# Leftover keys in four row groups, second weights' sums from their pieces, and a new order of the work

## The chip, the cores and the metric

The kernel runs on one core of a Trainium2 chip. The metric is the device time of one execution in microseconds. A core has TensorE (PE, with its weight loads shown apart as PEld), VectorE (DVE), ScalarE (ACT), GpSimd (POOL) and SyncE (SP), which here issues nearly all DMAs. Of TensorE's two clock levels, 1.2 and 2.4 GHz, this profile shows the upper one, a granted clock of 1.0, in every stretch.

## The reference

Attention over pooled keys and values, then a two-layer feed-forward with an own activation:

```python
# q, k, v: (8, 8, 576, 64) float32
k_p = k.reshape(B, H, 72, 8, D).mean(axis=3)          # 576 keys pooled by 8 to 72
v_p = v.reshape(B, H, 72, 8, D).mean(axis=3)
scores = q @ k_p.transpose(0, 1, 3, 2) / 8
attn = exp(scores - max); attn = attn / (attn.sum(-1) + 1e-9)
x = (attn @ v_p).transpose(0, 2, 1, 3).reshape(4608, 512)
h = x @ w_in                                           # (4608, 2048)
sp = maximum(h, 0) + log1p(exp(-abs(h)))
out = (h * erf(sp)) @ w_out                            # (4608, 512)
```

## The kernel before, in words

**Chunks and units.** The 4608 tokens are nine chunks of 512. A chunk's attention is made in two units of 256 tokens, 18 units in all; a unit is two tiles of 128 tokens. 576 tokens of a batch are no multiple of 256, so a unit may hold tokens of two batches (`parts`); those units read two sets of values.

**Precision.** Feed-forward operands are split into a high and a low part (`halves`, L460 and L472: `hi` is rounded, `lo` is the rest), and a product is three matmuls (`three`, L834: hi·hi, hi·lo, lo·hi). `pairs` issues them with 512 moving columns.

**A unit of attention.** `softmax_tile` makes the scores (L663), the softmax, and transposes the probabilities (L708). The 72 keys of a head are 64 plus 8 left over. The 64 of every head go through `pa` into `et`; the 8 left over are copied into the small tile `bb` (L460 or L461), transposed as a tile of their own (L709) into `pb`, and come out as `etb`, high and low part (L725, L726). `together` (L750) then multiplies by the values. It has two loops: L758, 16 matmuls for a part, 64 rows by 64 columns each, over the 64 keys; and L766, 8 matmuls for a part, 64 rows by 128 columns, over the leftover keys, whose values `vb` are a masked copy (L628: times the 0/1 columns `C_MB` over 8) in a high and a low part. Both loops add into two PSUM banks `pds`; each bank has two head pairs side by side, 256 columns each. The result is copied out, 256 columns at a time (L466 on ACT, L467 on DVE; for chunk 0 L781 and L782).

**Feed-forward.** Chunk 0 is multiplied plainly while the weights arrive: `load_in` and `load_out` load a weight tile, split it and store the split pieces to HBM (`in_hbm`, `out_hbm`) for later use, and for some tiles also the float32 tile itself (`raw_hbm`, L541 and L551). The other eight chunks go by pairs, s = 1 to 4. The first layer of a pair is eight `quad`s of seven products instead of eight (a Strassen-Winograd scheme), the second layer of the pairs 2 to 4 (`seconds`) likewise; pair 1 does its second layer plainly (`second`, L974), first one chunk with the weights in falling order, then the other in rising order.

**The sums.** The seven products need sums of the blocks of a weight tile. `sums(w, i, due)` (L554) loads two float32 tiles from `raw_hbm` (L560, tile `sw`), makes four sums of 128x256 (L566 to L569), splits them and stores them to HBM. For the second weights (w = 1) it runs during the second layer of pair 1.

**Order.** The functions only declare operations. A planner in the kernel (`Program`) orders them before anything is issued: it simulates the engines with the cost given for each operation, hands out the 8 PSUM banks (by kind, `CAPS`: "att" 4, "h" 6, "o" 4) and 84 places of SBUF, picks the engine where two are allowed (`both`, `copy`, `out_of_bank`), and after eight passes shifts the due times by the random moves in `MOVES`, one seed each. Every engine then works strictly in that order. The scores of a unit, its transposes and `together` stand between the products on PE.

Of the kernel before, what the change touches and what calls it, by code (L numbers as in the profile page):

```python
# [11 lines left out]
F32 = mybir.dt.float32  # L12
# [71 lines left out]
        "h": 6, "o": 4, "att": 4, "cv": 3, "dl": 3, "p1": 8}  # L84
# [14 lines left out]
def constants():  # L99
    c = np.zeros((P, C_N), np.float32)  # L100
    r = np.arange(P)
    c[:, C_ID:C_ID + P] = np.eye(P)
    c[:, C_MA] = -(r % 64 // 32)
    for p in range(NP):
        c[:, C_MB + p] = (r % 32 // 8 == p) / POOL
    for i, v in enumerate([-EC, 1 / 64 - 0.5]):
        c[:, C_BI + i] = v
    return c
# [301 lines left out]
def moe_attention(ctx: ExitStack, tc: tile.TileContext, cst, qa, kl, vl, wi, wo, out):  # L410
# [85 lines left out]
    raw_hbm = [[hbm.tile([P, 512], F32, tag=f"wf{w}{ft}", name=f"wf{w}{ft}") for ft in range(NJ)] for w in range(2)]  # L496
# [4 lines left out]
    RAW = [[Kept() for _ in range(NJ)] for _ in range(2)]  # L501
# [29 lines left out]
    def load_in(ft, due):  # L531


        f, hi, lo = convert(wi[ft], due, "fk" if ft % NQ >= NQ - KEPT else "f0")
        if ft % NQ >= NQ - KEPT:
            stays[ft] = f
        else:
            op("SP", 760, due + STORE, lambda: nc.sync.dma_start(raw_hbm[0][ft], f.ap), [f], [RAW[0][ft]])
        a = slice(0, 2) if ft < NQ else slice(1, 2)
        for l, w in enumerate((hi, lo)):  # L540
            op("SP", 760 if ft < NQ else 380, due + STORE + 1, lambda l=l, w=w: nc.sync.dma_start(  # L541
                f32(in_hbm[ft][:, a, l]), f32(w.ap).rearrange("p (a f) -> p a f", a=2)[:, a]), [w], [(IN[ft], l)])
        return hi, lo

    def load_out(ft, due):
# [5 lines left out]
        op("SP", 760, due + STORE + 1, lambda: nc.sync.dma_start(raw_hbm[1][ft], f.ap), [f], [RAW[1][ft]])  # L551
        return hi, lo

    def sums(w, i, due):  # L554
# [4 lines left out]
        for t, ft in () if kept else ((fb, i + NQ), (fa, i)):  # L559
            op("SP", 760, due - 4, lambda t=t, ft=ft: nc.sync.dma_start(t.ap, raw_hbm[w][ft]), [RAW[w][ft]], [t], ss, turn="s")  # L560
# [5 lines left out]
        add(due - 2.0, lambda e: e.tensor_add(sv[0](), h(*a21), h(*a22)), [a21[0], a22[0]], [S[0]])  # L566
        add(due - 1.9, lambda e: e.tensor_sub(sv[1](), sv[0](), h(*a11)), [a11[0], S[0]], [S[1]])
        add(due - 1.8, lambda e: e.tensor_sub(sv[2](), h(*a11), h(*a21)), [a11[0], a21[0]], [S[2]])
        add(due - 1.7, lambda e: e.tensor_sub(sv[3](), h(*a12), sv[1]()), [a12[0], S[1]], [S[3]])  # L569
# [47 lines left out]
    def values(b, base, due):  # L617
# [3 lines left out]
        vs, vb = buf("vs", [NP + 1, D]), buf("vb", [2, NP, D], F32R)  # L621
        values_of[b] = vs, vb
        n = P * D * POOL
        for p in range(NP + 1):
            load_pool(vl[b, n * p:n * p + n], lambda p=p: vs.ap[:, p, :], (vs, p),
                      base + VALS + VALS_R * p, "v", (D,), b < 1)
        vm = place("vm", F32, (NP, D))
        both(b < 2, dve(4 * D), gps(4 * D), due + VALS_S, lambda e: e.tensor_mul(  # L628
            vm.ap, vs.ap[:, NP].unsqueeze(1).broadcast_to([P, NP, D]),
            c[:, C_MB:C_MB + NP].unsqueeze(2).broadcast_to([P, NP, D])), [(vs, NP)], [vm])  # L630
        copy(b < 2, 4 * D, due + VALS_S, lambda: vb.ap[:, 0], lambda: vm.ap, [vm], [(vb, 0)])
        both(b < 2, dve(4 * D), gps(4 * D), due + VALS_S, lambda e: e.tensor_sub(
            vb.ap[:, 1], vm.ap, f32(vb.ap[:, 0])), [vm, (vb, 0)], [(vb, 1)])

    def unit(ck, u0, tiles, parts, moment):
# [9 lines left out]
        def softmax_tile(at, r):  # L645
# [7 lines left out]
            m, z, bb = buf("m", [H]), buf("z", [H]), buf("bb", [2, 2, NP, SP - 64])  # L653
# [52 lines left out]
            def turn():  # L706
                for p in range(NP):
                    nc.tensor.transpose(pa.ap[:, P * p:P * p + T], s.keys[:T, p, SP - 64:SP + 64], ident[:T, :T])  # L708
                nc.tensor.transpose(pb.ap[:, c0:c0 + T], bb.ap[:T].rearrange("t x y p k -> t (x y p k)"), ident[:T, :T])  # L709
# [3 lines left out]
            for y in range(2):  # L713
                copy(True, 64, r + 1.6, lambda y=y: bb.ap[:T, :, y], ends, [s], [(bb, y)])
# [29 lines left out]
    def together(ck, off, parts, due, plain, etb, et):  # L744
# [3 lines left out]
        pds = [bank("att") for _ in range(2)]  # L748
        srcs = [(*values_of[b], slice(o - off, o - off + m)) for b, o, m, _ in parts]

        def go():

            for i in range(2):
                for k, (vs, vb, es) in enumerate(srcs):
                    for y in range(2):
                        for x, pd in enumerate(pds):
                            h, p = slice(64 * x, 64 * x + 64), 2 * i + y
                            nc.tensor.matmul(pd.ap[64 * y:64 * y + 64, 256 * i + es.start:256 * i + es.stop],  # L758
                                             vs.ap[h, p], et.ap[h, p, es], start=i == 0 and k == 0, stop=False,
                                             skip_group_check=True)  # L760
            for i in range(2):
                for vs, vb, es in srcs:
                    for l in range(2):
                        for x, pd in enumerate(pds):
                            h = slice(64 * x, 64 * x + 64)
                            nc.tensor.matmul(pd.ap[:, 256 * i + es.start:256 * i + es.stop],  # L766
                                             vb.ap[h, l, 2 * i:2 * i + 2].rearrange("k y d -> k (y d)"),
                                             etb.ap[h, 1, es], start=False, stop=l == 1, skip_group_check=True)

        op("PE", 1583 + 350 * (len(srcs) - 1), due, go, [et, (etb, 1), *(t for vs, vb, _ in srcs for t in (vs, vb))], pds, step=True)  # L770
        for p in range(NP):
            pv, c0 = pds[p // 2], 256 * (p % 2)
# [344 lines left out]
    for s in range(1, NC // 2 + 1):  # L1117
# [10 lines left out]
        if s == 1:  # L1128
            for i in range(NQ):
# [54 lines left out]
```

## Time and profile before

| | us |
|---|---|
| median of three runs | 785.34 |
| range of the runs | 784.95 to 786.88 |
| the profiled execution | 784.27 |
| its span (first to last instruction) | 782.1 |
| PE busy | 768.4 |
| DVE busy | 659.5 |
| ACT busy | 528.7 |
| POOL busy | 379.5 |

A matmul's recorded time includes the pipe that follows its columns, so neighbours overlap and a busy PE is not PE at its peak. Queue q1 moved 206.62 MB.

### The profile page before, as it was taken

The page shows a single profiled execution, that of the slowest core. Times are in us where ns is not written, and L with a number is a line of the kernel's source. Part 1 is how long each engine was busy: PE and PEld are TensorE (multiplying, and loading weights), DVE is VectorE, ACT ScalarE, POOL GpSimd, SP SyncE. Part 2 cuts the span into 40 slices and gives each one's busy share as a digit, 9 for nine tenths or more (in the row PEclk, how much of TensorE's full clock was granted, in tenths as well). Part 3 has the DMA queues.
Part 4 walks back from the last instruction along what each step waited for, and adds up shares of the span by engine and source line. Part 5 has one row for each costly group of instructions (what it writes and reads, how often), then busy time and mean ns, then how long its engine had stood idle before and what let it go on. Part 6 is the DMA issues. An engine that isn't in the chain of part 4 may idle for free.

```text
span 782.1 us, 15122 instructions
## 1 busy us (share of the span) xinstructions
PE 768.4 (98%) x5158; PEld 660.6 (84%) x5158; DVE 659.5 (84%) x1143; ACT 528.7 (68%) x817; POOL 379.5 (49%) x367
## 2 busy tenths in 40 slices
PE   6999999999999999999999999999999999999998
PEld 5887888888888888888888888888888888888887
DVE  6989899868998981899999998799899937778972
ACT  3899994799967741688765445899754528887630
POOL 4978972397677100475735161757732404442220
PEclk9999999999999999999999999999999999999999
DMA  9989979999998998984591789833654788357551
GB/s 321 390 292 333 359 276 319 308 350 368 381 379 284 349 354 325 355 325 157 162 318 54 272 293 327 321 124 124 232 173 158 248 305 300 135 166 263 177 187 56
DMA packets 125292, 207.66 MB, mean 265 GB/s; under 512 B 12320, under 2 KB 44448, under 8 KB 125216
## 3 DMA queue, kind: packets, MB, share of 16 engines
q1 hardware_dynamic: 125072, 206.62, 76.0%
q8 instruction: 42, 0.69, 0.4%
q14 instruction: 34, 0.28, 0.1%
q10 hardware_dynamic: 144, 0.07, 0.0%
HBM read 160.50 MB, written 46.14 MB: 264 GB/s over the span
## 4 chain that ended last, share of the span: by engine, by line
PE 90%; DMA 5%; DVE 3%; POOL 1%; issue 1%; ACT 0%; SPq 0%; DVEq 0%; POOLq 0%; ACTq 0%
PE o L834 44%; PE h L834 37%; PE att L663 2%; PE att L758 2%; PE att L708 2%; DMA ws<-ws 2%; PE att L766 2%; DMA v<-vl 1%; DMA q<-qa 1%; DMA w<-wi 1%; PE att L709 0%; DMA cst<-cst 0%; DVE ks L604 0%; DVE g L861 0%; DVE gl L472 0%
## 5 line engine op out<-in xcount | busy, mean ns | idle before, releaser
L834 PE MATMUL o<-gl,w 128*128 128x512 f32 x1536 | 339.6, 381 | 0.0
L834 PEld LDWEIGHTS o<-gl,w 128*128 128x128 f32 x1536 | 288.3, 189 | 41.4 <-issue 0.4
L834 PE MATMUL h<-x,w 128*128 128x512 f32 (+1 forms) x1392 | 300.0, 374 | 3.4 <-POOL w L472 0.9
L834 PEld LDWEIGHTS h<-x,w 128*128 128x128 f32 x1392 | 253.7, 189 | 40.6 <-DVE t L941 1.8
L861 POOL TENSOR_TENSOR g<-d,g 128x512 f32<-128x512 f32 x65 | 86.0, 1336 | 124.0 <-ACT d L857 63.9
L472 DVE TENSOR_TENSOR gl<-g,gl 128x512 fp32r<-128x512 f32 x174 | 131.6, 781 | 3.7 <-POOL gl L461 3.2
L460 ACT ACTIVATE gl<-g 128x512 fp32r<-128x512 f32 x173 | 100.0, 622 | 33.3 <-DVE gl L472 10.9
L1004 POOL TENSOR_TENSOR g<-g 128x512 f32<-128x512 f32 x41 | 60.4, 1472 | 50.6 <-DVE gl L472 20.0
L941 DVE TENSOR_TENSOR g<-t,h 128x512 f32<-128x512 f32 x96 | 65.6, 683 | 21.5 <-PE h L834 20.7
L857 ACT ACTIVATE d<-d 128x1024 f32<-128x1024 f32 x72 | 73.5, 1053 | 0.4
L853 ACT ACTIVATE d<-g 128x512 f32<-128x512 f32 x103 | 59.3, 622 | 6.3 <-DVE g L941 6.2
L853 ACT ACT_TABLE_LOAD x43 | 55.2, 1283 | 11.4 <-PE h L834 10.1
L472 POOL TENSOR_TENSOR gl<-g,gl 128x512 fp32r<-128x512 f32 x34 | 49.2, 1452 | 23.4 <-ACT gl L460 22.7
L941 DVE TENSOR_TENSOR t<-t,h 128x512 f32<-128x512 f32 x57 | 39.1, 686 | 21.6 <-PE h L834 19.3
L857 ACT ACT_TABLE_LOAD x40 | 51.3, 1283 | 0.7
L461 POOL TENSOR_SCALAR gl<-g 128x512 fp32r<-128x512 f32 x35 | 32.1, 922 | 32.4 <-PE o L834 12.8
L460 ACT ACTIVATE x<-xr 128x512 fp32r<-128x512 f32 (+2 forms) x57 | 30.6, 557 | 24.1 <-DVE xr L808 15.8
L691 ACT ACTIVATE s<-s,cst 128x576 f32<-128x576 f32 x36 | 27.5, 769 | 27.1 <-DVE s L687 27.0
L834 PE MATMUL h<-x,ws 128*128 128x512 f32 x192 | 43.1, 379 | 0.0
L834 PEld LDWEIGHTS h<-x,ws 128*128 128x128 f32 x192 | 36.3, 189 | 5.1
L604 DVE TENSOR_REDUCE ks<-k 128x64 f32<-128x512 f32 (+1 forms) x40 | 24.2, 624 | 18.7 <-DMA k<-kl 18.6
L1004 DVE TENSOR_TENSOR g<-g 128x512 f32<-128x512 f32 x55 | 39.3, 732 | 0.3
(105 smaller groups left out, 930.2 us busy)
## 6 DMA issues: line engine op xcount, KB each, us to landing
w<-ws SPq DMA_DIRECT2D x192, 256.0 KB, 5.2
w<-wo SPq DMA_DIRECT2D x128, 256.0 KB, 4.5
w<-wi SPq DMA_DIRECT2D x96, 256.0 KB, 5.2
ws<-ws SPq DMA_DIRECT2D x64, 256.0 KB, 4.8
v<-vl SPq DMA_DIRECT2D x40, 256.0 KB, 5.3
q<-qa SPq DMA_DIRECT2D x36, 256.0 KB, 5.3
out<-f SPq DMA_DIRECT2D x35, 256.0 KB, 2.6
k<-kl SPq DMA_DIRECT2D x32, 256.0 KB, 5.2
```

The costliest lines, as they stand in the source:

```text
L460: op("ACT", act(n), prio, lambda: nc.scalar.activation(dst(), src(), AF.Copy, scale=scale), *access, turn=turn, alt=("POOL", gps1(n), lamb ...
L461: alt=("POOL", gps1(n), lambda: nc.gpsimd.tensor_scalar(out=dst(), in0=src(), scalar1=scale, scalar2=0.0, op0=ALU.mult, op1=ALU.add)) if p ...
L472: both(True, dve(n), gps(n), prio + 0.1, lambda e: e.tensor_sub(lo(), src(), f32(hi())), reads + [hikey], [lokey])
L604: op("DVE", dve(8 * n), prio, lambda: nc.vector.tensor_reduce(to(), t.ap, AX.X, ALU.add), [t], [t, key], alt=("POOL", gps(4 * n) + gps(2 * ...
L663: nc.tensor.matmul(pss[x].ap[r0:r0 + 64, SP * p:SP * p + SP], raw.ap[h:h + 64, p, r0:r0 + 64], ks.ap[h:h + 64, p], start=p == 0, stop=True ...
L691: op("ACT", act(H * SP) + 93, r + 0.8, lambda: nc.scalar.activation(s.keys[:T], s.keys[:T], AF.Sigmoid, bias=bias[0][:T], scale=1.0 / 64.0 ...
L834: nc.tensor.matmul(o, u, v, start=first and q == 0, stop=last and q == 2, skip_group_check=True)
L853: nc.scalar.activation(y(k), hs[k][0].ap, AF.Softplus)
L857: op("ACT", act(1024), prio + 0.2, lambda k=k: nc.scalar.activation(ys[k].ap, ys[k].ap, AF.Erf), own[2 * k:2 * k + 2], own[2 * k:2 * k + 2 ...
L861: both(True, dve(512), gps(512), prio + 0.3, lambda e, k=k, h=h: e.tensor_mul(h.ap, y(k), h.ap), [own[k], h], [h])
L941: op("DVE", dve(512), prio, lambda: nc.vector.tensor_add(dst.ap, u.ap, o.ap), [u, o], [dst])
L1004: both(True, dve(512), gps(512), prio, lambda e: e.tensor_sub(out.ap, u.ap, v.ap), [u, v], [out])
```

## The change

The leftover keys are laid out so that each bank's two head pairs have 32 rows of their own: `bb` is ordered (half, pair, copy, key). The loop at L766 then gives eight matmuls for a part of 32 rows by 128 columns, two in each of four row groups, each row group into a PSUM bank of its own; the results of a unit lie in four banks, 256 columns in each. `vm` and `vb` have two blocks in place of four. The float32 second weights are no longer stored to HBM and loaded again: where pair 1's second layer has the pieces of two weight tiles at hand, they are added, high and low, in halves of 256 columns (32 additions, DVE or POOL), and `sums` takes these. "att" may hold 6 banks. The planner's cost of `together` is another, and the list of moves has 590 seeds in place of 308.

```diff
 MOVES = (
-    5777643, 29890795, 49640867,
...
+    59118814, 93230492, 30119130,
...
-        "h": 6, "o": 4, "att": 4, "cv": 3, "dl": 3, "p1": 8}
+        "h": 6, "o": 4, "att": 6, "cv": 3, "dl": 3, "p1": 8}
...
-    c[:, C_MA] = -(r % 64 // 32)
-    for p in range(NP):
-        c[:, C_MB + p] = (r % 32 // 8 == p) / POOL
+    c[:, C_MA] = -(r % 16 // 8)
+    for p in range(2):
+        c[:, C_MB + p] = (r % 32 // 16 == p) / POOL
...
-        op("SP", 760, due + STORE + 1, lambda: nc.sync.dma_start(raw_hbm[1][ft], f.ap), [f], [RAW[1][ft]])
         return hi, lo
-    def sums(w, i, due):
+    def sums(w, i, due, pieces=None):
...
-        for t, ft in () if kept else ((fb, i + NQ), (fa, i)):
+        for t, ft in () if kept or pieces else ((fb, i + NQ), (fa, i)):
...
+        for t, ps in zip((fa, fb), pieces or ()):
+            for m, p in enumerate(ps):
+                both(True, dve(256), gps(256), due - 2.5, lambda e, t=t, m=m, p=p: e.tensor_add(
+                    t.ap[:, 256 * m:256 * m + 256], f32(p.ap[:, 0]), f32(p.ap[:, 1])), [p], [(t, m)])
...
-        vm = place("vm", F32, (NP, D))
+        vm = place("vm", F32, (2, D))
...
-            m, z, bb = buf("m", [H]), buf("z", [H]), buf("bb", [2, 2, NP, SP - 64])
+            m, z, bb = buf("m", [H]), buf("z", [H]), buf("bb", [2, NP, 2, SP - 64])
...
-        pds = [bank("att") for _ in range(2)]
+        pds = [bank("att") for _ in range(NP)]
...
-            for i in range(2):
-                for vs, vb, es in srcs:
-                    for l in range(2):
-                        for x, pd in enumerate(pds):
-                            h = slice(64 * x, 64 * x + 64)
-                            nc.tensor.matmul(pd.ap[:, 256 * i + es.start:256 * i + es.stop],
-                                             vb.ap[h, l, 2 * i:2 * i + 2].rearrange("k y d -> k (y d)"),
-                                             etb.ap[h, 1, es], start=False, stop=l == 1, skip_group_check=True)
-        op("PE", 1583 + 350 * (len(srcs) - 1), due, go, ...
+            for vs, vb, es in srcs:
+                for l in range(2):
+                    for p, pd in enumerate(pds):
+                        h = slice(32 * p, 32 * p + 32)
+                        nc.tensor.matmul(pd.ap[:, es], vb.ap[h, l].rearrange("k y d -> k (y d)"), etb.ap[h, 1, es],
+                                         start=False, stop=l == 1, skip_group_check=True)
+        op("PE", 1360 + 230 * (len(srcs) - 1), due, go, ...
...
-            for i in range(NQ):
-                sums(1, i, start(s) + LONG + 4 + i * (span - 4) / NQ)
...
                     second(2 * s - 1 + t, k, due, ws[k], half_row, 0 if t else NJ - 1, NJ - 1 if t else 0)
+                    i = k // 2
+                    if k % 2 == t and i % 2 != t:
+                        sums(1, i, due + 3, (ws[2 * i], ws[2 * i + 1]))
```

## Rows read from the trace of the kernel before

**Rows 1.** The page's first parts: busy time of each engine; granted clock.

```profile
PE 768.4 (98%) x5158; PEld 660.6 (84%) x5158; DVE 659.5 (84%) x1143; ACT 528.7 (68%) x817; POOL 379.5 (49%) x367
...
PEclk9999999999999999999999999999999999999999
```

**Rows 2.** PE alone by stretches: stretch, length, PE busy, clock, DMA share, GB/s.

```profile
25.30:80.00 54.70, 52.32 (x485) 1.00 0.92 330
80.00:180.00 100.00, 99.97 (x632) 1.00 0.95 325
180.00:212.00 32.00, 31.43 (x200) 1.00 1.05 375
212.00:778.00 566.00, 565.98 (x3593) 1.00 0.70 241
```

**Rows 3.** Chain that ended last, 0 to 30 us: start, length, what.

```profile
10.62 8.42 DMA v<-vl
...
23.13 1.78 DVE ks L604 x3
...
25.95 1.49 PE h L834 x11
```

**Rows 4.** Timeline of PE, a one-part and a two-part unit: start, length, instructions.

```profile
96.19 0.74 PE L766 MATMUL att<-etb,vb 64*128 64x256 f32 x8
96.86 0.70 PE L834 MATMUL o<-gl,w 128*128 128x512 f32 x2
...
241.70 1.08 PE L766 MATMUL att<-etb,vb 64*128 64x192 f32 x16
242.71 0.66 PE L758 MATMUL att<-et,vs 64*64 64x256 f32 x8
```

**Rows 5.** The same engine, 17 to 31 us: filler matmuls of 256 columns, and a unit's L758.

```profile
18.22 2.57 PE L1144 MATMUL att<-cst 128*128 128x256 bf16 x22
...
27.93 1.04 PE L758 MATMUL att<-et,vs 64*64 64x256 f32 x16
```

**Rows 6.** Line L766: all its matmuls by form.

```profile
L766 PE MATMUL att<-etb,vb x192: 212/276/384, 21.8 to 596.6; 64*128 64x256 f32 x96, 64*128 64x64 f32 x32, 64*128 64x192 f32 x32, 64*128 64x128 f32 x32
```

**Rows 7.** L766 by stretches (columns: length; PE busy, count; PEld busy, count; clock, DMA share, GB/s).

```profile
79.60:135.00 55.40, 2.59 (x32) 2.04 (x32) 1.00 0.93 317
...
204.00:305.00 101.00, 3.30 (x40) 2.57 (x40) 1.00 1.00 351
...
392.00:471.00 79.00, 1.85 (x24) 1.50 (x24) 1.00 0.68 237
...
555.00:640.00 85.00, 1.48 (x16) 1.07 (x16) 1.00 0.65 218
```

**Rows 8.** Lines L551 and L560, stores and loads of float32 tiles: issue ns min/median/max, times.

```profile
L551 SPq DMA_DIRECT2D wf<-f x16: 430/660/1907, 108.8 to 169.1; - x16
...
L560 SPq DMA_DIRECT2D sw<-wf x20: 319/402/1087, 175.0 to 270.3; - x20
```

**Rows 9.** Line L566: additions of 128x256, ns min/median/max.

```profile
L566 DVE TENSOR_TENSOR sw<-sw x8: 409/418/426, 180.6 to 283.0; 128x256 f32<-128x256 f32 x8
...
L566 POOL TENSOR_TENSOR sw<-sw x2: 731/732/732, 233.6 to 249.0; 128x256 f32<-128x256 f32 x2
```

**Rows 10.** All engines, 210 to 305 us: length; PE, PEld, DVE, ACT, POOL busy, clock, DMA share, GB/s.

```profile
210.00:305.00 95.00, 94.98 (x717) 80.80 (x716) 78.37 (x157) 54.23 (x107) 36.37 (x38) 1.00 1.00 348
```

**Rows 11.** Groups of instructions by line: xcount | busy us, mean ns | idle before.

```profile
L834 PE MATMUL o<-gl,w 128*128 128x512 f32 x1536 | 339.6, 381 | 0.0
...
L466 ACT COPY xr<-att 128x256 f32<-128x256 f32 x37 | 12.1, 379 | 17.0 <-PE att L766 14.7 <-DVE xr L467 2.2
...
L467 DVE COPY xr<-att 128x256 f32<-128x256 f32 x27 | 10.3, 417 | 2.3 <-PE att L766 1.4 <-ACT xr L466 0.7
```

More of the change, by code (lines that the diff above doesn't have):

```diff
@@ L495, in moe_attention @@
     in_hbm = [hbm.tile([P, 2, 2, 256], F32R, tag=f"wi{ft}", name=f"wi{ft}") for ft in range(NJ)]
-    raw_hbm = [[hbm.tile([P, 512], F32, tag=f"wf{w}{ft}", name=f"wf{w}{ft}") for ft in range(NJ)] for w in range(2)]
+    raw_hbm = [hbm.tile([P, 512], F32, tag=f"wf{ft}", name=f"wf{ft}") for ft in range(NJ)]
     sum_hbm = [[[hbm.tile([P, 2, 2, 256], F32R, tag=f"ws{w}{i}{m}", name=f"ws{w}{i}{m}") for m in range(2)]
@@ L500, in moe_attention @@
     IN, OUT = ([Kept() for _ in range(NJ)] for _ in range(2))
-    RAW = [[Kept() for _ in range(NJ)] for _ in range(2)]
+    RAW = [Kept() for _ in range(NJ)]
     SUM = [[[Kept() for _ in range(2)] for _ in range(NQ)] for _ in range(2)]
@@ L537, in load_in @@
         else:
-            op("SP", 760, due + STORE, lambda: nc.sync.dma_start(raw_hbm[0][ft], f.ap), [f], [RAW[0][ft]])
+            op("SP", 760, due + STORE, lambda: nc.sync.dma_start(raw_hbm[ft], f.ap), [f], [RAW[ft]])
         a = slice(0, 2) if ft < NQ else slice(1, 2)
@@ L558, in sums @@
         ss = [place("sw", shape=(2, 256)) for _ in range(2)]
-        for t, ft in () if kept else ((fb, i + NQ), (fa, i)):
-            op("SP", 760, due - 4, lambda t=t, ft=ft: nc.sync.dma_start(t.ap, raw_hbm[w][ft]), [RAW[w][ft]], [t], ss, turn="s")
+        for t, ft in () if kept or pieces else ((fb, i + NQ), (fa, i)):
+            op("SP", 760, due - 4, lambda t=t, ft=ft: nc.sync.dma_start(t.ap, raw_hbm[ft]), [RAW[ft]], [t], ss, turn="s")
+        for t, ps in zip((fa, fb), pieces or ()):
+            for m, p in enumerate(ps):
+                both(True, dve(256), gps(256), due - 2.5, lambda e, t=t, m=m, p=p: e.tensor_add(
+                    t.ap[:, 256 * m:256 * m + 256], f32(p.ap[:, 0]), f32(p.ap[:, 1])), [p], [(t, m)])
         h = lambda t, k: t.ap[:, 256 * k:256 * k + 256]
@@ L565, in sums @@
         S = [(ss[j // 2], j % 2) for j in range(4)]
[L566 to L569, printed above, removed]
+        add(due - 2.0, lambda e: e.tensor_add(sv[0](), h(*a21), h(*a22)), [a21, a22], [S[0]])
+        add(due - 1.9, lambda e: e.tensor_sub(sv[1](), sv[0](), h(*a11)), [a11, S[0]], [S[1]])
+        add(due - 1.8, lambda e: e.tensor_sub(sv[2](), h(*a11), h(*a21)), [a11, a21], [S[2]])
+        add(due - 1.7, lambda e: e.tensor_sub(sv[3](), h(*a12), sv[1]()), [a12, S[1]], [S[3]])
         got = []
@@ L617, in values @@
     def values(b, base, due):
-        vs, vb = buf("vs", [NP + 1, D]), buf("vb", [2, NP, D], F32R)
+        vs, vb = buf("vs", [NP + 1, D]), buf("vb", [2, 2, D], F32R)
         values_of[b] = vs, vb
@@ L626, in values @@
                       base + VALS + VALS_R * p, "v", (D,), b < 1)
-        vm = place("vm", F32, (NP, D))
[L628 to L632, printed above, removed]
+        vm = place("vm", F32, (2, D))
+        both(b < 2, dve(2 * D), gps(2 * D), due + VALS_S, lambda e: e.tensor_mul(
+            vm.ap, vs.ap[:, NP].unsqueeze(1).broadcast_to([P, 2, D]),
+            c[:, C_MB:C_MB + 2].unsqueeze(2).broadcast_to([P, 2, D])), [(vs, NP)], [vm])
+        copy(b < 2, 2 * D, due + VALS_S, lambda: vb.ap[:, 0], lambda: vm.ap, [vm], [(vb, 0)])
+        both(b < 2, dve(2 * D), gps(2 * D), due + VALS_S, lambda e: e.tensor_sub(
             vb.ap[:, 1], vm.ap, f32(vb.ap[:, 0])), [vm, (vb, 0)], [(vb, 1)])
@@ L708, in turn @@
                     nc.tensor.transpose(pa.ap[:, P * p:P * p + T], s.keys[:T, p, SP - 64:SP + 64], ident[:T, :T])
-                nc.tensor.transpose(pb.ap[:, c0:c0 + T], bb.ap[:T].rearrange("t x y p k -> t (x y p k)"), ident[:T, :T])
+                nc.tensor.transpose(pb.ap[:, c0:c0 + T], bb.ap[:T].rearrange("t x p y k -> t (x p y k)"), ident[:T, :T])
             ends = lambda: s.keys[:T].rearrange("t p (x k) -> t x p k", k=SP - 64)[:, 0::2 * SP // (SP - 64) - 1]
             for y in range(2):
-                copy(True, 64, r + 1.6, lambda y=y: bb.ap[:T, :, y], ends, [s], [(bb, y)])
+                copy(True, 64, r + 1.6, lambda y=y: bb.ap[:T, :, :, y], ends, [s], [(bb, y)])
             pav = lambda: pa.ap.rearrange("p (a t) -> p a t", t=P)[:, :, :T]
@@ L755, in go @@
                     for y in range(2):
-                        for x, pd in enumerate(pds):
+                        for x in range(2):
                             h, p = slice(64 * x, 64 * x + 64), 2 * i + y
-                            nc.tensor.matmul(pd.ap[64 * y:64 * y + 64, 256 * i + es.start:256 * i + es.stop],
-                                             vs.ap[h, p], et.ap[h, p, es], start=i == 0 and k == 0, stop=False,
-                                             skip_group_check=True)
-            for i in range(2):
-                for vs, vb, es in srcs:
-                    for l in range(2):
-                        for x, pd in enumerate(pds):
-                            h = slice(64 * x, 64 * x + 64)
-                            nc.tensor.matmul(pd.ap[:, 256 * i + es.start:256 * i + es.stop],
-                                             vb.ap[h, l, 2 * i:2 * i + 2].rearrange("k y d -> k (y d)"),
-                                             etb.ap[h, 1, es], start=False, stop=l == 1, skip_group_check=True)
-        op("PE", 1583 + 350 * (len(srcs) - 1), due, go, [et, (etb, 1), *(t for vs, vb, _ in srcs for t in (vs, vb))], pds, step=True)
+                            nc.tensor.matmul(pds[2 * x + i].ap[64 * y:64 * y + 64, es], vs.ap[h, p], et.ap[h, p, es],
+                                             start=k == 0, stop=False, skip_group_check=True)
+            for vs, vb, es in srcs:
[4 more added lines that the diff above has]
+                                         start=False, stop=l == 1, skip_group_check=True)
+        op("PE", 1360 + 230 * (len(srcs) - 1), due, go, [et, (etb, 1), *(t for vs, vb, _ in srcs for t in (vs, vb))], pds, step=True)
         for p in range(NP):
-            pv, c0 = pds[p // 2], 256 * (p % 2)
+            pv, c0 = pds[p], 0
             r = due + p * 0.4
@@ L1162 @@
     va = np.stack([v6[:, 0, :, SP - 64:], v6[:, 1, :, :64]], axis=2).reshape(B, NP, P, POOL, D)
-    vb = np.stack([v6[:, 0, :, :SP - 64], v6[:, 1, :, 64:]], axis=1).reshape(B, 2, 1, NP * (SP - 64), POOL, D)
-    vr = np.concatenate([va, np.concatenate([vb, vb], axis=2).reshape(B, 1, P, POOL, D)], axis=1)
+    vb = np.stack([v6[:, 0, :, :SP - 64], v6[:, 1, :, 64:]], axis=1)
+    vr = np.concatenate([va, np.stack([vb, vb], axis=3).reshape(B, 1, P, POOL, D)], axis=1)
     kt = kr.swapaxes(-1, -2)
```

76 rows, old and new, of the table MOVES are left out of this document.

## The prediction

> **What bounds the kernel now.** I read the page's first parts, then PE alone by stretches, then the chain that ended last, and at the end single units on the timeline. PE is busy for 768.4 of 782.1 us at a granted clock of 1.0 throughout, the level of 2.4 GHz [rows 1]. Busy alone says little, so look at how little is missing: from 25.3 to 80 us 2.38 us, from 80 to 180 us 0.03, from 180 to 212 us 0.57, and from 212 to 778 us 0.02 [rows 2]. So there are three stretches. Up to 25.3 us PE waits for the opening; the chain goes through a transfer of values, reductions on DVE and the first operand, and the first long run of products starts at 25.95 us [rows 3]. From there to 212 us PE loses 3.0 us in a few gaps. After that it never waits: other engines and transfers can be late only within their slack, and time is won by giving PE less to do, and by nothing else. A gap in the busy time understates the loss: a product is recorded with 381 ns [rows 11], while 512 columns follow each other every 339.6/1536 = 221 ns, so up to 0.16 us of each gap is covered by the pipe of the last matmul. With some six to eight gaps the loss is about 4 us.
>
> **Leftover keys.** Line L766 has 192 matmuls, 96 of them with 256 columns: at 8 for a part these are 12 units of one part and 6 of two parts (16 matmuls each) [rows 6]. A one-part unit's block takes 96.86 - 96.19 = 0.67 us, a two-part unit's 242.71 - 241.70 = 1.01 us [rows 4]. What does one matmul of 256 columns take by itself? The fillers: (2.57 - 0.16)/22 = 0.11 us [rows 5]. Eight of them one after another would be 0.88 us, so two row groups run side by side now, four pairs of 0.11 us and 0.23 us around them. After the change the same eight matmuls lie in four row groups with a bank each. If four run at once, there are two rounds in place of four: 2 x 0.11 = 0.22 us less. In a two-part unit a pair takes (1.01 - 0.23)/8 = 0.098 us, and four of eight rounds go: 0.39 us less. One of the one-part units comes before the first product (25.3 us) and saves nothing; 11 x 0.22 + 6 x 0.39 = 4.8 us, all of it on PE's path.
>
> The bounds: above, if a block is nothing but its rounds, half of it goes, 11 x 0.335 + 6 x 0.505 = 6.7 us. Below, if only two of the 32-row matmuls run at once, nothing goes. If they ran one at a time, eight would take 0.88 and sixteen 1.76 us, 11 x 0.21 + 6 x 0.75 = 6.8 us more; I exclude that, since two row groups overlap in these rows, and in L758 16 matmuls in two row and two column groups take 1.04 us with 256 columns [rows 5], less than the 1.76 us of one at a time. I take 4.8 us, for four at a time is what L758's time is nearest to.
>
> The Trainium skill (TensorE: Matmul & The Clock Gate, section "Part 3: Packing small matmuls") gives 3.07 times for four row groups of 32 rows with 512 columns, not four. No row here shows four row groups, so the trace neither agrees nor disagrees. By that, an estimate, a round would be 0.14 us and this term 11 x 0.16 + 6 x 0.27 = 3.4 us.
>
> **Four banks, and the smaller values tile.** `together` needs four free banks where it needed two. It reads `et` and `etb`, so the unit's own transposed banks have been copied out by then; two more than before have to be free. The copies out stay 256 columns each, 0.38 us on ACT or 0.42 us on DVE [rows 11], and each bank is released by one copy where two released it. What waits in PE's line behind a late bank is every product that follows; the cover is that products of other banks can be placed ahead of it, and PE had no gap from 212 us on [rows 2]. I take 0; without the cover it is the third rival. `vm` and `vb` are halved on DVE, ACT and POOL, eight batches, off PE's path: 0 on the sum.
>
> **Sums from the pieces.** All 16 stores of float32 second weights (109 to 169 us) and 16 of the 20 loads (up to 270 us) go [rows 8]: 32 transfers of 256 KB, each also an issue on SP. They lie where the DMA share is about 1.0, but PE loses 0.03 us from 80 to 180 and 0.02 us after 212 us [rows 2], so what they delay was already in time: 0. A gain of at most the 0.57 us of 180 to 212 us is possible, since transfers are nearest to being late there. Added are 32 additions of 128x256: at 0.42 us on DVE 13.4 us, at 0.73 us on POOL 23.4 us [rows 9]. From 210 to 305 us DVE has 95.0 - 78.4 = 16.6 us free and POOL 58.6 us [rows 10], and the summed weights are wanted only by the next pair: 0. If that cover were gone (all on DVE, ahead of the splits that PE waits for), 13.4 us is the ceiling, less what POOL takes. The pieces are held a little longer in their places; the loads behind them wait for that on SP, which has the removed issues' time to make it up.
>
> **New order.** PE's order and everything else's is dealt out anew; nothing in the trace of before gives a price for it. It can at best win the 3 to 4 us of gaps between 25 and 212 us, and some of the opening, where I allow 1 us either way (a DVE group of the chain, such as the three reductions of 1.78 us [rows 3], may be put earlier or later). It can also open new gaps: by the same rows as much again, 4 us, where the bank kinds are filled anew. I take a gain of 1.5 us, nearer to none than to all, because PE lost these gaps in the stretch where all engines are full and which the change touches little.
>
> **The sum**, against the profiled execution of 784.27 us: -4.8 (leftover keys) - 1.5 (gaps) + 0 (sums, banks) = -6.3, 778.0 us. The median is 785.34, 1.1 us above that execution, so I predict a median of 779.0 us.
>
> **Rivals.**
>
> 1. The 32-row groups run two at a time, or the new round is twice as long. Then only the gaps' 1.5 us come: 783.8 us. For it: no row shows four row groups. Against it: L758 overlaps four 64x64 blocks, and banks differ for all four groups.
>
> 2. The new order closes nearly all gaps and moves the opening up by 1 us: -4.8 - 3.5 - 1 = -9.3, 776.0 us. For it: the gaps are few and long, so few rearrangements would do. Against it: up to 80 us all engines are nearly full.
>
> 3. Slower: the banks. Where four banks hold the second layer's outputs, only four are left, and `together` takes them all. By L766's stretches that is three units at 80 to 135 us (32 matmuls), four at 204 to 305 (40), two at 392 to 471 (24) and two at 555 to 640 (16): 11 units [rows 7]. If PE waits at each for the last two banks to be copied out, one after the other on one engine, 2 x 0.42 = 0.84 us, and the scores behind it wait again for as much, it loses 11 x 1.7 = 18 us; with one wait 9.2 us. Net of the 4.8 us and without the gaps' gain this gives 789.8 us for one wait. It decides from 4.8/11 = 0.44 us a unit, about one copy. For it: the Trainium skill (TensorEngine Tiling (Array Packing), section "Restrictions and Gotchas") says that row tiles have to write to different banks and so press on PSUM; the trace of before has two row groups with a bank each, as that wants. Against it: PE has gone through these very stretches without a gap, and copies out were in time.
>
> 4. The leftover keys bring their 4.8 us, and the new order gives back 3 to 4 us in new gaps, in the opening or where the pieces are held: 784.0 us.
>
> **How the numbers follow.** Forecast 0.55 (777 to 781.5 us), all gaps closed 0.18 (776), two at a time 0.08 (783.8), gaps given back 0.12 (half of it under 783 us), banks 0.07 (789.8). A measurement of this kernel tells 0.3%, 2.4 us, from no change: under 783.0 us is faster, over 787.7 us slower. Faster: 0.55 + 0.18 + 0.06 + a fifth of 0.08 = 0.81; slower: nearly all of the banks' case, 0.06; the rest, 0.13, is the same. The range leaves out the banks, the upper end of the two cases beside it, and what lies under the upper bound of 6.7 us with all gaps closed: 775.5 to 784.0 us.
>
> **What would show it.** Leftover keys: L766 blocks of about 0.45 us (one part) and 0.62 us (two parts) in place of 0.67 and 1.01; if they stay, the first step is wrong. Gaps: PE's missing time between 25 and 212 us at 1 to 2 us less, the first product within 1 us of 25.3. Banks: no wait of PE at L758 or L663 for a copy out, and nothing missing after 212 us; 5 us missing there would make the prediction wrong. Sums: the additions on DVE or POOL without PE waiting, and 8.4 MB less on the queue.

## The result

The changed kernel takes 778.73 us (median; 778.18 to 779.06), the kernel before 785.54 us beside it: a ratio of 0.991, 95% interval 0.9893 to 0.9927, so 6.8 us less. The forecast was 779.0 us, faster. The profiled execution took 779.06 us with a span of 777.3 us; against the profiled execution of before (784.27 and 782.1 us) that is 5.2 and 4.8 us less. Before's profiled execution was 1.3 us under its median, the changed kernel's 0.3 us above, so the rows below have to account for 4.8 us and not for 6.8. Beside the later runs the kernel before had medians of 784.86, 785.33, 785.34 and 786.67 us; a difference between medians of two sessions is good to about 1 us.

In the changed kernel L785 is the old L758, L791 the old L766, L690 the scores, L735 and L736 the transposes, L858 the products. The page's first part, as in [rows 1]:

```profile
PE 764.9 (98%) x5145; PEld 654.5 (84%) x5145; DVE 656.8 (85%) x1150; ACT 530.1 (68%) x811; POOL 415.5 (53%) x400
```

PE alone by stretches, columns as in [rows 2]:

```profile
25.30:80.00 54.70, 53.39 (x478) 1.00 0.93 316
80.00:180.00 100.00, 99.70 (x643) 1.00 0.98 331
180.00:212.00 32.00, 32.00 (x178) 1.00 0.94 309
212.00:773.00 561.00, 560.46 (x3609) 1.00 0.69 232
```

PE misses 1.31, 0.30, 0.00 and 0.54 us, 2.15 us in all, where before it missed 3.0 [rows 2]. The stretch up to 80 us lost less than before, that up to 212 us nothing; small gaps opened between 80 and 180 us and at 224 us, in the second layer of pair 1.

PE's timeline at a one-part and a two-part unit, to be laid beside [rows 4], and at the first product, beside [rows 3]:

```profile
24.61 0.38 PE L858 MATMUL h<-x,w 128*128 128x256 f32 x1
25.29 0.96 PE L858 MATMUL h<-x,w 128*128 128x256 f32 x6 [0.30 <-DVE x L806]
...
98.00 0.38 PE L858 MATMUL o<-gl,w 128*128 128x512 f32 x1
98.31 1.09 PE L785 MATMUL att<-et,vs 64*64 64x256 f32 x16
99.33 0.51 PE L791 MATMUL att<-etb,vb 32*128 32x256 f32 x8
99.77 0.73 PE L858 MATMUL o<-gl,w 128*128 128x512 f32 x2
...
249.12 0.64 PE L791 MATMUL att<-etb,vb 32*128 32x192 f32 x16
249.68 0.48 PE L858 MATMUL o<-gl,w 128*128 128x512 f32 x1
```

Take each block from its start to the start of what follows: 99.77 - 99.33 = 0.44 us for one part and 249.68 - 249.12 = 0.56 us for two, where it was 0.67 and 1.01 [rows 4]. All blocks of the line together, in the view of groups by line (count | busy us, mean ns), the kernel before and the changed one: 15.5 us and 10.1 us.

```profile
L766 PE MATMUL att<-etb,vb 64*128 64x256 f32 (+3 forms) x192 | 15.5, 291 | 0.0
L791 PE MATMUL att<-etb,vb 32*128 32x256 f32 (+3 forms) x192 | 10.1, 306 | 0.3 <-DVE z L725 0.3
```

The sums' part: 4 loads of float32 tiles are left of 20 [rows 8], the 32 additions are there (20 on DVE, 12 on POOL, at the durations of [rows 9]), and q1 moves 198.23 MB where it moved 206.62.

```profile
L583 SPq DMA_DIRECT2D sw<-wf x4: 399/502/617, 158.4 to 178.1; - x4
...
L586 DVE TENSOR_TENSOR sw<-w x20: 406/410/955, 210.9 to 289.8; 128x256 f32<-128x256 f32 x20
L586 POOL TENSOR_TENSOR sw<-w x12: 717/730/1182, 191.7 to 256.4; 128x256 f32<-128x256 f32 x12
```

All engines from 210 to 305 us (length; PE, PEld, DVE, ACT, POOL; clock, DMA share, GB/s): DVE has 6 us left, where it had 16.6 [rows 10], and the DMA share fell from 1.00 to 0.88.

```profile
210.00:305.00 95.00, 94.46 (x748) 79.75 (x747) 89.05 (x181) 51.03 (x100) 44.78 (x50) 1.00 0.88 285
```

What PE waited for (us in total, times, longest), the largest:

```profile
PE att L1168 <- DMA cst<-cst: 3.8, 1, 3.8
PE att L735 <- POOL s L728: 1.3, 2, 1.0
PE att L736 <- ACT bb L484: 0.7, 2, 0.4
PE att L736 <- POOL bb L485: 0.5, 1, 0.5
```

No row of PE has `together` or the scores wait for a copy out of a bank. Of the weight loads (PEld), those of L785 name the copies on ACT (L490) three times, 0.3 us each, which is what a load waits there without a cause too (3.0 us at nine times).

### The profile page after: what moved, and what is told of

Read it like the earlier page. It is cut to its first block, busy times and chain, and to the rows that moved or that the text cites. A ratio compares the mean times of both kernels' runs of the same rounds, so it can differ in the third digit from the quotient of the medians.

```text
span 777.3 us, 15064 instructions
## 1 busy us (share of the span) xinstructions
PE 764.9 (98%) x5145; PEld 654.5 (84%) x5145; DVE 656.8 (85%) x1150; ACT 530.1 (68%) x811; POOL 415.5 (53%) x400
## 3 DMA queue, kind: packets, MB, share of 16 engines
q1 hardware_dynamic: 120464, 198.23, 75.7%
## 4 chain that ended last, share of the span: by engine, by line
PE 85%; POOL 2%; DVE 2%; DMA 1%; issue 0%; SPq 0%; ACT 0%; DVEq 0%; POOLq 0%
PE o L858 41%; PE h L858 37%; PE att L785 2%; PE att L690 2%; PE att L735 2%; PE att L791 1%; POOL w L496 1%; DMA v<-vl 1%; DMA wi<-w 0%; PE att L736 0%; POOL bb L485 0%; POOL low L544 0%; DVE gl L496 0%; DVE sw L586 0%; DVE g L885 0%
## 5 line engine op out<-in xcount | busy, mean ns | idle before, releaser
L858 PE MATMUL o<-gl,w 128*128 128x512 f32 x1536 | 341.8, 381 | 0.8 <-DVE s L714 0.5
L858 PEld LDWEIGHTS o<-gl,w 128*128 128x128 f32 x1536 | 287.5, 189 | 42.8 <-POOL w L496 1.7
L858 PE MATMUL h<-x,w 128*128 128x512 f32 (+1 forms) x1392 | 299.7, 374 | 1.0 <-DVE s L714 0.5
L858 PEld LDWEIGHTS h<-x,w 128*128 128x128 f32 x1392 | 254.2, 189 | 36.7 <-PE att L690 0.6
L885 POOL TENSOR_TENSOR g<-d,g 128x512 f32<-128x512 f32 x65 | 83.8, 1305 | 95.0 <-ACT d L881 86.2
L484 ACT ACTIVATE gl<-g 128x512 fp32r<-128x512 f32 x179 | 105.1, 622 | 32.6 <-PE o L858 10.4
L496 DVE TENSOR_TENSOR gl<-g,gl 128x512 fp32r<-128x512 f32 x165 | 121.2, 762 | 2.6 <-POOL gl L485 1.5
L496 POOL TENSOR_TENSOR gl<-g,gl 128x512 fp32r<-128x512 f32 x43 | 68.4, 1596 | 39.1 <-ACT gl L484 37.7
L485 POOL TENSOR_SCALAR gl<-g 128x512 fp32r<-128x512 f32 x29 | 41.8, 1442 | 38.7 <-PE o L858 17.7
L1028 POOL TENSOR_TENSOR g<-g 128x512 f32<-128x512 f32 x33 | 43.6, 1321 | 28.1 <-DVE g L1028 9.5
L484 ACT ACTIVATE x<-xr 128x512 fp32r<-128x512 f32 (+2 forms) x51 | 28.3, 569 | 41.2 <-DVE xr L832 29.1
L1028 DVE TENSOR_TENSOR g<-g 128x512 f32<-128x512 f32 x63 | 43.4, 709 | 0.4
L858 PE MATMUL h<-x,ws 128*128 128x512 f32 x192 | 43.2, 379 | 0.0
L485 POOL TENSOR_SCALAR bb<-s 128x64 f32<-128x64 f32 x45 | 15.8, 364 | 49.9 <-DVE s L728 42.5
L858 PEld LDWEIGHTS h<-x,ws 128*128 128x128 f32 x192 | 36.3, 189 | 5.2
```

The lines of the kernel that those rows point to most:

```text
L484: op("ACT", act(n), prio, lambda: nc.scalar.activation(dst(), src(), AF.Copy, scale=scale), *access, turn=turn, alt=("POOL", gps1(n), lamb ...
L485: alt=("POOL", gps1(n), lambda: nc.gpsimd.tensor_scalar(out=dst(), in0=src(), scalar1=scale, scalar2=0.0, op0=ALU.mult, op1=ALU.add)) if p ...
L496: both(True, dve(n), gps(n), prio + 0.1, lambda e: e.tensor_sub(lo(), src(), f32(hi())), reads + [hikey], [lokey])
L858: nc.tensor.matmul(o, u, v, start=first and q == 0, stop=last and q == 2, skip_group_check=True)
L885: both(True, dve(512), gps(512), prio + 0.3, lambda e, k=k, h=h: e.tensor_mul(h.ap, y(k), h.ap), [own[k], h], [h])
L1028: both(True, dve(512), gps(512), prio, lambda e: e.tensor_sub(out.ap, u.ap, v.ap), [u, v], [out])
```

## The experiments

The runs ask two things: whether a shorter block is a shorter time, and how much of the rest belongs to the sums and how much to the order.

**The leftover matmuls twice** (e2). Engine orders as in the changed kernel, PE alone has more.

```diff
-                for l in range(2):
+                for l in (0, 0, 1, 1):
                     for p, pd in enumerate(pds):
```

> The changed kernel with each of the leftover keys' matmuls issued twice (their share of the result counts twice). Theory (each round is on PE's path): two more rounds of 0.11 us in a one-part unit, four of 0.1 us in a two-part unit, 11 x 0.22 + 6 x 0.4 = 4.8 us longer, 783.5 us. Rival (the units' time is hidden behind other waits): under 1 us longer.

Measured: 783.55 us (782.81 to 784.52), ratio to the kernel before 0.9981 (0.9968 to 0.9994). PE's timeline at the same two units:

```profile
99.46 0.74 PE L791 MATMUL att<-etb,vb 32*128 32x256 f32 x16
100.14 0.48 PE L858 MATMUL o<-gl,w 128*128 128x512 f32 x1
...
250.83 1.08 PE L791 MATMUL att<-etb,vb 32*128 32x192 f32 x32
251.85 0.92 PE L858 MATMUL o<-gl,w 128*128 128x512 f32 x3
```

Sixteen matmuls now take 0.68 us and thirty-two 1.02 us: what eight and sixteen took before [rows 4]. The two added rounds of a one-part unit are (0.68 - 0.44)/2 = 0.12 us each, the four of a two-part unit (1.02 - 0.56)/4 = 0.115 us. So four matmuls of 32 rows take what two of 64 rows took, and this kernel is the changed one with the old length of its blocks. Its 4.8 us over the changed kernel are the leftover keys' share in this order; what it stays under the kernel before is all the rest: 1.3 us beside the 784.86 us of that kernel in the same session, 2.0 us beside the 785.54 us of the result. What sets the price of a round stays open: by the recorded starts of the two-part unit at 120.2 us, rounds of 64 columns follow each other after 0.133, 0.111 and 0.112 us, so a quarter of the columns does not make a round cheaper.

**The loops swapped** (e1).

```diff
-                for l in range(2):
-                    for p, pd in enumerate(pds):
+                for p, pd in enumerate(pds):
+                    for l in range(2):
                         h = slice(32 * p, 32 * p + 32)
```

> The changed kernel with the two inner loops of the leftover keys swapped: the same eight matmuls of 32 rows for a part, but the high and the low part of one row group follow each other, and then the next row group. Engine orders, banks and transfers as in the changed kernel. Theory (the gain is four row groups at once, and all of it lies on PE's path): five rounds of 0.11 us in place of two, blocks of about 0.77 us (one part) and 1.0 us (two parts) in place of 0.44 and 0.6; 11 x 0.33 + 6 x 0.4 = 6.0 us longer, about 784.7 us. Rival (a 32-row matmul is cheap by itself, or PE has slack for it): blocks or at least the time as before, 778.7 us.

Measured: 778.89 us (778.6 to 780.61). PE's timeline, the same one-part unit:

```profile
99.39 0.52 PE L791 MATMUL att<-etb,vb 32*128 32x256 f32 x8
99.84 0.72 PE L858 MATMUL o<-gl,w 128*128 128x512 f32 x2
```

The block takes 0.45 us, as if nothing had been swapped. The recorded starts of its eight matmuls say why: 0, 7, 14, 20, then 222, 230, 237 and 243 ns, where the unswapped one has 0, 3, 6, 10, 223, 225, 229, 233. Four matmuls still start together, and they are one of each row group: the fifth, seventh and eighth by start carry the semaphore increments that others wait for, as in the unswapped kernel, and in the order of issue these would be the second, sixth and eighth. So the second matmul of a row group, issued between them, did not hold up the next group, and PE does not start matmuls strictly in the order of issue within this block. The expectation of five rounds was wrong, and this run does not separate four at a time from two. Starts alone do not either (those of L758 in the kernel before come in fours too, but 0.22 us apart); the price of a round in e2 does.

**32 added transfers** (e3 and e5). Beside each of the two stores of a second weight's pieces one more transfer of 256 KB in the same SP operation: in e3 a store of the piece, in e5 an HBM-to-HBM copy of input data.

```diff
...
             op("SP", 760, due + STORE, lambda l=l, w=w: nc.sync.dma_start(
                 f32(out_hbm[ft][:, :, l]), f32(w.ap).rearrange("p (a f) -> p a f", a=2)), [w], [(OUT[ft], l)])
+            op_last = pr.ops[-1]
+            op_last.fn = lambda l=l, w=w, first=op_last.fn: (first(), nc.sync.dma_start(dead_hbm[l][ft], f32(w.ap)))
+            op_last.choice = {"SP": (op_last.cost, op_last.fn)}
```

In e5 the added source is another:

```diff
-            op_last.fn = lambda l=l, w=w, first=op_last.fn: (first(), nc.sync.dma_start(dead_hbm[l][ft], f32(w.ap)))
+            op_last.fn = lambda l=l, w=w, first=op_last.fn: (first(), nc.sync.dma_start(
+                dead_hbm[l][ft], kl[l, P * 512 * (ft % 4):P * 512 * (ft % 4 + 1)].rearrange("(p x) -> p x", p=P)))
```

> The changed kernel with 32 more stores of 256 KB to HBM that nobody reads, two beside the stores of each tile of the second weights: as many bytes as the sums' change took off the queue (8.4 MB), put where the old stores were. Theory (the removed transfers delayed nothing that was late): within 0.3% of 778.7 us, under 1 us longer, PE's missing time from 80 to 212 us as in the changed kernel. Rival (the queue is full there and its relief was part of the gain): 25 us of full queue, of which a tenth or more reaches PE, 2.5 us or more longer.

> The changed kernel with 32 added transfers of 256 KB at the same places in SP's order as the 32 added stores, but from HBM to HBM, of input data that no engine touches: the same issues on SP and as many bytes, no place in SBUF held longer. Theory A (the added stores cost 18 us because the tiles that they read come free later, and other engines wait for these): within 2 us of 778.8 us. Theory B (the queue's time itself is short between 87 and 180 us, and the transfers behind come late): 788 us or more, with PE missing time at 140 to 212 us.

Measured: e3 796.74 us (794.45 to 798.3), e5 796.44 us (794.98 to 797.55); 18 us over the changed kernel both, so the theory of e3 (under 1 us) was wrong and theory B of e5 right. That e5 costs the same excludes held tiles as the cause: it is that later transfers come late. PE by stretches in e5, then the two ends of its longest wait on PE's timeline, and the wait of DVE before it:

```profile
80.00:140.00 60.00, 59.72 (x453) 1.00 1.04 374
140.00:180.00 40.00, 35.08 (x154) 0.96 1.01 346
180.00:212.00 32.00, 25.82 (x107) 0.89 0.97 335
```

```profile
183.65 1.46 PE L863 MATMUL h<-x,w 128*128 128x512 f32 x6
186.97 1.28 DVE L636 TENSOR_REDUCE ks<-k 128x64 f32<-128x512 f32 x2 [7.71 <-DMA k<-kl]
191.29 2.93 PE L863 MATMUL h<-x,w 128*128 128x512 f32 x6 [6.18 <-DVE t L970]
```

The DMA share is about 1.0 from 80 to 212 us, and PE misses 4.9 and 6.2 us in the last two stretches; in the changed kernel, with 0.95, 1.02 and 0.94, it missed nothing there, so a share of 1.0 does not tell by itself that PE will wait. The clock adds to it: after 6.18 us without work the six products take 2.93 us where the six before the wait took 1.46, the lower of the two clock levels, and the mean granted clock of the stretch is 0.89. DVE in turn stood still for 7.71 us until a tile of keys had landed (L636), and its work for PE lies behind that in its order. This load was issued at 180.95 us, 14.9 us later than in the changed kernel, and landed 6.0 us after its issue, where it took 5.8 us there. SP issues its other transfers in the same order in both kernels, and falls behind step by step: by 4 us when 8 of the added transfers are issued, by 11 us with 26, by 14 to 15 us with all 32. Each added issue takes SP 0.63 us, 20 us in all. So the delay arises in SP's line of issues; whether SP's own issuing time is the limit, or the DMA engines that it feeds at a share of 1.0, these runs do not separate, since they add both.

**16 added transfers** (e6): e5 with one copy a tile, as many as the old stores, issued from 96.7 to 158.6 us, where the old ones were issued from 108.8 to 169.1 [rows 8].

```diff
+            if l:
+                continue
             op_last = pr.ops[-1]
```

> The changed kernel with 16 of the 32 added HBM-to-HBM transfers of 256 KB, one beside each tile of the second weights: as many as the old stores, and at their place. Theory A (each transfer on the full queue costs PE about 18/32 = 0.55 us from the first on): 787 to 788 us. Theory B (there is slack first: the kernel before carried 16 stores there with 0.03 us of PE missing): under 782 us.

Measured: 785.15 us over ten runs (782.48 to 788.65), 6.4 us over the changed kernel, between the two theories, and its runs spread over nearly all that lies between them; the ratio to the kernel before is 0.9991 (0.9973 to 1.0008). On the mean a transfer costs 0.4 us here and 0.56 us in e5; whether the first few are free, no run shows.

**The parts alone, with the planner's order and no moves** (n1 to n4).

```diff
-MOVES = (
...
+MOVES = ()
```

> The kernel before with an empty list of moves: the planner's order after its eight passes. It is the base for the three kernels run beside it. Both theories: slower than 785.3 us by what the searched moves are worth, 4 us or more, most of it as missing PE time up to 212 us.

> The kernel before with the leftover keys' part of the change alone, empty list of moves. Theory (four row groups at once save 4.8 us on PE's path, four banks cost nothing): 4 to 6 us under the same kernel before without moves. Rival (the gain came from the order or the sums): within 1.5 us of it.

> The kernel before with the sums' part of the change alone, empty list of moves. Theory of the prediction (what the removed transfers delayed was in time): within 1.5 us of the kernel before without moves. Rival (the queue is tight between 100 and 212 us, as the 32 added stores showed): 2 us or more under it.

> The changed kernel with an empty list of moves. Theory: under the kernel before without moves by the sum of the two parts, 5 to 6 us; the distance to the changed kernel with its moves is within 1.5 us of that of the kernel before to its own. Rival (the new order is most of the gain): the distance to the kernel before without moves is under 3 us.

**The same with searched moves** (s1 to s3): one search with the planner's own simulated length as its measure, equal time for each. It kept 47, 129 and 42 moves, where the own lists have 308 (before) and 590 (changed).

> The kernel before with another list of moves, searched with the same effort for this and the two kernels beside it. It is the base for these. Between 785.5 (its own list) and 804.4 us (none).

> The leftover keys' part alone with a searched list of moves. Theory (4.8 to 5 us on PE's path, whatever the order): 3 to 7 us under the searched kernel before. Rival (its 9.2 us without moves is its worth, since fewer 64-row matmuls also ease the order): 8 us or more under it.

> The whole change with a searched list of moves. Theory A (the sums' part is worth nothing once the order is tuned): within 1.5 us of the leftover keys' part alone. Theory B (its freed queue time is worth 2 to 5 us, as without moves): 2 us or more under it.

Measured, medians in us (the kernel before beside them took 786.67 and 785.34):

| | no moves | searched here | own moves |
|---|---|---|---|
| kernel before | 804.43 | 797.12 | 785.5 |
| leftover keys alone | 795.23 | 792.76 | |
| sums alone | 799.86 | | |
| whole change | 792.60 | 793.38 | 778.7 |

PE from 25.3 to 770 us, in the order n1, n2, n3, n4, s1, s2, s3; one fence for each kernel:

```profile
25.30:770.00 744.70, 730.95 (x4783) 0.99 0.76 261
```

```profile
25.30:770.00 744.70, 735.32 (x4849) 1.00 0.77 264
```

```profile
25.30:770.00 744.70, 732.55 (x4798) 1.00 0.74 252
```

```profile
25.30:770.00 744.70, 733.52 (x4836) 1.00 0.74 254
```

```profile
25.30:770.00 744.70, 735.57 (x4828) 1.00 0.77 265
```

```profile
25.30:770.00 744.70, 734.91 (x4841) 1.00 0.77 265
```

```profile
25.30:770.00 744.70, 733.53 (x4827) 1.00 0.74 254
```

In each of these PE misses 9 to 14 us (744.70 less its busy time); with the kernels' own moves it misses 3.0 (before) and 2.15 us (changed). The own moves are worth 18 us to the kernel before (18.9 against 785.5 us, 17.8 against the 786.67 us beside it) and 13.9 to the changed one, more than the change.

The leftover keys' part comes out at 9.2 us (n1 to n2), 7.3 (n3 to n4) and 4.4 (s1 to s2), the sums' part at 4.6 (n1 to n3), 2.6 (n2 to n4) and -0.6 (s2 to s3), the whole change at 11.8 and 3.7, with the 6.8 us of the kernels as they are between. The leftover blocks behind the first product, added up on PE's timeline from each one's start to the start of what follows, save nearly the same in each pair: 5.1, 5.1 and 4.9 us. The rest is gaps that fall otherwise, and the clock behind them. Three examples: n1 misses 4.4 us more than n2; the first product of s2 starts at 32.34 us, that of s1 at 26.29; and the mean granted clock in n1 is 0.97 from 25.3 to 80 us and 0.95 from 140 to 212, which by an estimate from these is 0.03 x 54.7 + 0.05 x 72 = 5 us, while in s1 it is 1.00 throughout. The 4.4 us are also uncertain by themselves, since the four runs of s1 lie between 793.4 and 798.74 us. So most expectations of n2 to n4 were missed (4 to 6 us for the leftover keys, within 1.5 us for the sums, 5 to 6 us for the whole), those of s2 (3 to 7 us) and s3 (theory A) were met; that the change is worth 5 to 6 us in any order was wrong, and the searched orders made no fairer base: good by the planner's simulation, they were 12 to 15 us behind the kernels' own on the chip.

## Why the prediction was right

**Leftover keys, -4.8 us: right in size and in mechanism.** Blocks of 0.45 and 0.62 us were forecast; 0.44 us and 0.56 us stand in the rows (by the recorded starts the six two-part blocks take 0.57 to 0.63 us). Five of the six took 1.01 to 1.07 us before, so by the blocks it is 11 x 0.23 + 6 x 0.44 = 5.2 us, by e2 4.8 us of time. Rival 1 falls. But why the prediction took four at a time was wrong: L758's time is not nearest to that. By the prediction's own sum, its 16 matmuls would take 4 x 0.11 + 0.23 = 0.67 us four at a time and 8 x 0.11 + 0.23 = 1.11 us two at a time, and 1.04 us were recorded [rows 5]. Nothing in the rows of before decided between two and four, and that the choice came true was luck. The Trainium skill's 3.07 times for four row groups (TensorE: Matmul & The Clock Gate, "Part 3: Packing small matmuls") would have given a round of 0.14 us; e2's rounds of 0.115 to 0.12 us, no longer than those of two row groups, say four at the price of one with 256 columns, and the measurement decides. The same section lets matmuls start strictly in program order; the swapped loops, where the first matmuls of all four groups start ahead of the second of any, do not agree with it across row groups.

**Four banks, 0: right, as far as the rows show it.** No wait of PE names a copy out of a bank, and PE misses 0.5 us after 212 us, at one place, where a transpose waits for a leftover tile from POOL. Rival 3 falls.

**Gaps and opening, -1.5 us: -1.2 us, but taken back elsewhere, and the median met by luck.** The first product starts 0.7 us earlier, and behind it PE's gaps are 2.5 us where they were 3.0 (the 0.85 us between the stretches leaves out a gap of 0.30 us before 25.3). With the blocks that makes 6.4 us, and the span fell by 4.8. The difference lies in what PE issues. Added up on PE's timeline from start to start, gaps apart, the leftover blocks take 5.2 us less, but the 3170 products 1.2 us more (682.2 and 683.5) and the scores 1.3 us more; the loop over the 64 keys takes 0.6 us and the transposes take 0.3 us less. The products' part is probably that of the seams: between the first product and the last the products stand in 58 stretches where they stood in 49. In the rows above the last product before L785 starts 0.31 us ahead of it where 0.22 would do, and the two products after L791 are recorded with 0.73 us where 0.22 + 0.38 would do; before a transpose, which like a product uses all 128 rows and columns, nothing is lost (0.216 us). This is read from rows, no run tested it, and why the scores took longer stays open. Neither was a term of the sum, and together they took back what the gaps and the opening gave. So the forecast for the execution, 778.0 us, was 1.1 us too low. The median still came out right, because the prediction carried over the 1.1 us by which before's median lay above its execution, while the changed kernel's median lies 0.3 us below its own: two errors, of 1.1 and 1.4 us, that cancel.

**Sums, 0: not shown, and its reason does not carry over to a new order.** The argument was that transfers which delay nothing are free to remove. In the changed kernel's order 16 transfers near the place of the old stores cost 6.4 us and 32 cost 18: SP's line has little slack there. The kernel before carried its 16 stores there with PE missing 0.03 us; its order was made with them, and that of e6 was not, which is the likely reason. So freed time on the queue is probably worth something only to an order that uses it, and the rows of one order cannot price it. How much of the 1.3 to 2 us that e2 leaves is the freed queue and how much another draw of the order stays open: in three comparisons the sums' part changed the time by -4.6, -2.6 and +0.6 us. The additions cost nothing visible; DVE took 20 of them and had 6 us left in that stretch.

## What to carry to other kernels

When PE misses a few us of 780, price the change by the blocks that PE itself issues: count the rounds, and check with a run that doubles them. Here a round cost 0.11 to 0.12 us with two matmuls of 64 rows as with four of 32, so laying out the same work in four row groups, with a bank each, halved the rounds; whether each needs a bank of its own was not tested. Don't price a removed transfer, or a part of a change, with the order that was made around it: try it in several orders, and take the spread between them as the error. And when a forecast meets the median, check it against the profiled execution as well, term by term.

## What the runs showed that was not expected

- A matmul can start ahead of one of another row group that was issued before it: with the high and low part of each group issued one after the other, the first ones of four groups still started within 20 ns, and the block took 0.45 us as in the other order.
- With SP's line full, 16 added transfers of 256 KB cost 6.4 us and 32 cost 18 us, more than twice as much; a copy from HBM to HBM costs as much as a store from SBUF (796.44 and 796.74 us).
- The same program in other orders of the planner's making was 12 to 19 us slower, also in those that had been searched for.
